# Reordered first loads, single stores of q and k, and earlier weight slices in an adaLN transformer block

## The chip, the cores and the metric

The kernel runs on one core of one Trainium2 chip. Its time is the device time of one execution in microseconds. The core has five engines that run their own instruction streams: TensorE (PE in the profile; PEld is its weight load), VectorE (DVE), ScalarE (ACT), GpSimd (POOL) and SyncE (SP), which here issues all DMAs, in order.

## The reference

One block with adaptive layer norm: six modulation rows are made from a condition vector c. Attention with 32 heads of 16 follows, and a dense layer pair with Mish between. All is float32, with S = 2048 rows of D = 512.

```python
mod = (_silu(c) @ w_mod).reshape(c.shape[0], 6, 1, -1)
sa, ca, ga, sb, cb, gb = (mod[:, i] for i in range(6))      # written out in the original
h = _layernorm(x) * (1 + ca) + sa
x = x + ga * attention(h, wqkv, wo)      # softmax(q k^T * 16**-0.5) v, then @ wo
h = _layernorm(x) * (1 + cb) + sb
x = x + gb * dense(h, w1, b1, w2)        # (v * tanh(softplus(v))) @ w2 with v = h @ w1 + b1
```

## The kernel before

**Precision.** Most products are made from split operands: each factor is a high part (rounded to the matmul format, `hi_copy`) and a low part (the rest, `lo_sub`), and three products hi x hi, hi x lo and lo x hi are summed (`mm3`). `h_h` and `h_l` are the two parts of the normalised input, transposed; `wh` and `wl` those of a weight slice; `qh` and `ql` those of a q or k unit.

**The start** (lines 329 to 514). x is 16 tiles of 128 rows, or four blocks (`tb`) of 512 rows. SP loads c, the first two 512-column parts of w_mod (`wma`, 1 MB each), x tiles 0 to 3, a 128-column weight slice of k and one of q, and then the other x tiles with the v slice among them. `sil` is silu(c). TensorE multiplies it with `wma` (line 449), ScalarE copies the result, and 16 matmuls with one column each (line 455, against `sel`) sum it into `modc`, which holds shift and scale per feature. The layer norm of a block is: statistics on VectorE (`stats_tb`, lines 374 and 375; `first_norm` for block 0), a few small operations on GpSimd, the scaling of x in place on ScalarE (`apply_tb`, line 385), transposes on TensorE and then, in `tr_tb`, `h_h` from PSUM on ScalarE (line 440), the same value in full precision, `hf`, on VectorE (line 441), and `h_l` as their difference (line 101) on VectorE or GpSimd (`LOV` says which). For each block the k unit of heads 0 to 7 follows (for block 0 the q unit too), with its matmuls against `h_l` last; for blocks 1 and 2 two v units as well. ScalarE casts the v weight slice (line 94) ahead of that.

**The way through memory.** A q or k unit (`qk_unit`, 8 heads by 512 rows) is written to HBM, to `qscr` and `kscr`, in the layout that the score matmuls read. For each of the 16 features of a head q has the three rows hi, hi, lo, and k has hi, lo, hi, so that one matmul over 48 rows makes the sum of three products. Two more rows of q hold a shift by the row maximum (`mt`, line 577), set to zero at first (`constants`). So q takes 50 rows and k 48 rows a head. A k unit is stored with two DMAs (512 and 256 KB), a q unit with three of 256 KB. `load_q` and `load_k` fetch a pair of heads into rows 0 and 64 of a `qa` and a `ka` tile, with one DMA per head each; there are five tiles of each (`NR`).

**The steps.** After that an order written out by hand runs in steps t = -20 to 511 and half steps h = 2t. Hooks (`at(h, f)`) put loads, stores and small operations at half steps. An iteration n is 16 steps: four heads (pairs 2n and 2n+1) against 512 query rows. The row maxima of a pair (lines 553 and 555 in the first 20 steps, 539 and 541 later) run 20 steps ahead of its scores (line 588), exponentials (591) and products with v (606; one group of eight instructions a step). Units of q, k and v of other heads, and later the dense layers, fill TensorE beside that. Pair 2n+1 is loaded at h = 32(n-1), when the tile that it takes comes free, and its first maxima come at step 16n - 12, which is four steps later. Pairs 2 and 3 are loaded at h = -22 and -8.

**Early weight slices.** `early_prep` loads six 256 KB slices of w1, splits them on GpSimd and stores both parts in HBM (`w1scr`); the six are loaded at h = 3i - 37, split 7 and stored 10 half steps later. GpSimd also splits the q and k weight slices and q and k units of that stretch.

`free_banks` tells the scheduler which instructions on different PSUM banks do not depend on each other, by the tile names that they touch.

## Time and profile before

| | us |
|---|---|
| three runs | 1690.85, 1691.66, 1695.13 (median 1691.66) |
| the profiled execution | 1691.02 |
| its span in the trace | 1689.2 |
| TensorE busy in the span | 1667.3 |
| VectorE, ScalarE, GpSimd busy | 1441.5, 1355.1, 821.1 |

Times in the trace count from the start of the span. A busy TensorE is not TensorE at its peak, since matmuls are pipelined. A row of the trace in order of time has the start, the length, the engine, the line, the operation with its tiles (written <- read) and shapes, a count where equal rows were merged, and, in brackets, how long the engine was idle before and what released it. "SPq" rows are DMA issues: their length is the time that SP took to issue, not the transfer's.

### The profile page before, as it was taken

The page shows a single profiled execution, that of the slowest core. Times are in us where ns is not written, and L with a number is a line of the kernel's source. Part 1 is how long each engine was busy: PE and PEld are TensorE (multiplying, and loading weights), DVE is VectorE, ACT ScalarE, POOL GpSimd, SP SyncE. Part 2 cuts the span into 40 slices and gives each one's busy share as a digit, 9 for nine tenths or more (in the row PEclk, how much of TensorE's full clock was granted, in tenths as well). Part 3 has the DMA queues.
Part 4 walks back from the last instruction along what each step waited for, and adds up shares of the span by engine and source line. Part 5 has one row for each costly group of instructions (what it writes and reads, how often), then busy time and mean ns, then how long its engine had stood idle before and what let it go on. Part 6 is the DMA issues. An engine that isn't in the chain of part 4 may idle for free.

```text
span 1689.2 us, 33772 instructions
## 1 busy us (share of the span) xinstructions
PE 1667.3 (99%) x12418; PEld 921.5 (55%) x12418; DVE 1441.5 (85%) x2369; ACT 1355.1 (80%) x2612; POOL 821.1 (49%) x843
## 2 busy tenths in 40 slices
PE   7999999999999999999999999999999999999999
PEld 5755655555444455555555455555555455555687
DVE  8898888888989988888889888888889888883377
ACT  6257777777778998888888998888888998889674
POOL 7555224655313564556323564556323565555442
PEclk9999999999999999999999999999999999999999
DMA  7877556777755443434355434534354533533261
GB/s 248 269 244 199 147 150 185 218 223 216 231 142 146 110 94 98 117 88 129 84 137 152 115 77 93 139 77 127 87 144 122 130 94 77 144 107 132 75 230 63
DMA packets 115406, 238.98 MB, mean 141 GB/s; under 512 B 24928, under 2 KB 50544, under 8 KB 109288
## 3 DMA queue, kind: packets, MB, share of 16 engines
q1 hardware_dynamic: 115240, 236.82, 49.9%
q8 instruction: 98, 1.61, 0.4%
q14 instruction: 68, 0.56, 0.1%
HBM read 180.48 MB, written 51.45 MB: 137 GB/s over the span
## 4 chain that ended last, share of the span: by engine, by line
PE 91%; DVE 3%; ACT 3%; DMA 2%; POOL 1%; issue 1%; SPq 0%; ACTq 0%; DVEq 0%; POOLq 0%
PE bk L606 29%; PE ring L588 22%; PE ring L539 20%; PE bk L139 11%; PE bk L132 3%; PE ring L1219 2%; PE ring L132 2%; DVE mx L541 2%; ACT pr L591 1%; PE ring L553 0%; DMA qa<-mt 0%; DMA xt<-in_A_x 0%; PE ring L922 0%; DMA kscr<-qh 0%; PE ring L568 0%
## 5 line engine op out<-in xcount | busy, mean ns | idle before, releaser
L541 DVE TENSOR_REDUCE mx<-ring 128x1 f32<-128x512 f32 x1968 | 1223.1, 682 | 150.0 <-PE ring L539 136.4
L591 ACT ACTIVATE pr<-ring 128x512 f32<-128x512 f32 x2048 | 1078.4, 603 | 207.1 <-PE bk L139 124.7
L539 PE MATMUL ring<-ka,qa 64*128 64x512 f32 x1968 | 817.9, 429 | 1.4 <-ACT pr L591 1.1
L588 PE MATMUL ring<-qa,ka 64*128 64x512 f32 x2048 | 759.1, 402 | 3.4 <-ACT pr L591 1.9
L606 PE MATMUL bk<-pr,vg 128*32 128x512 f32 x4096 | 545.1, 604 | 0.0
L539 PEld LDWEIGHTS ring<-ka,qa 64*128 64x128 f32 x1968 | 350.5, 184 | 326.2 <-DVE mx L541 251.3
L588 PEld LDWEIGHTS ring<-qa,ka 64*128 64x128 f32 x2048 | 373.7, 184 | 194.7 <-DVE mx L541 111.4
L139 PE MATMUL bk<-h,w 64*128 64x512 f32 (+1 forms) x1080 | 278.1, 390 | 0.0
L139 PE MATMUL bk<-w,a_h 64*128 64x512 f32 x632 | 210.9, 413 | 0.0
L139 PEld LDWEIGHTS bk<-h,w 64*128 64x128 f32 x1080 | 178.5, 184 | 9.3 <-ACT pr L591 1.5
L606 PEld LDWEIGHTS bk<-pr,vg 128*32 128x32 f32 x4096 | 81.2, 108 | 135.4 <-issue 126.0
L139 PE MATMUL bk<-w,a_l 64*128 64x512 f32 x316 | 124.0, 392 | 0.0
L139 PEld LDWEIGHTS bk<-w,a_h 64*128 64x128 f32 x632 | 106.8, 184 | 4.3 <-ACT hb L800 1.0
L978 POOL TENSOR_TENSOR y<-yd,y 128x512 f32<-128x512 f32 x44 | 56.9, 1293 | 89.0 <-ACT yd L977 79.7
L812 POOL TENSOR_SCALAR qq<-ee 128x512 f32<-128x512 f32 x25 | 15.5, 619 | 169.6 <-ACT ee L806 169.6
L828 POOL TENSOR_TENSOR qq<-qq,rr 128x512 f32<-128x512 f32 x42 | 54.1, 1289 | 85.9 <-ACT rr L822 85.9
L814 POOL TENSOR_TENSOR hb<-hb,ee 128x512 f32<-128x512 f32 x42 | 54.1, 1288 | 79.6 <-DVE ee L810 77.7
L139 PE MATMUL bk<-w,o_hl 64*128 64x512 f32 x288 | 79.1, 405 | 0.0
L101 POOL TENSOR_TENSOR a_l<-hb,a_h 128x512 fp32r<-128x512 f32 x53 | 73.1, 1379 | 4.4
L98 POOL TENSOR_SCALAR qh<-qf 128x512 fp32r<-128x512 f32 x27 | 16.7, 619 | 90.8 <-ACT qf L262 69.4
L139 PEld LDWEIGHTS bk<-w,a_l 64*128 64x128 f32 x316 | 58.3, 185 | 3.4
L139 PE MATMUL bk<-h_h,wl 64*128 64x512 f32 x168 | 57.2, 420 | 0.2 <-ACT pr L591 0.2
(219 smaller groups left out, 1909.1 us busy)
## 6 DMA issues: line engine op xcount, KB each, us to landing
ka<-kscr SPq DMA_DIRECT2D x124, 384.0 KB
w<-w2scr SPq DMA_DIRECT2D x56, 512.0 KB
w<-w1scr SPq DMA_DIRECT2D x46, 512.0 KB
vg<-vscr SPq DMA_DIRECT2D x32, 552.0 KB
qa<-qscr SPq DMA_DIRECT2D x124, 100.0 KB
kscr<-qh SPq DMA_DIRECT2D x16, 512.0 KB
qscr<-qh SPq DMA_DIRECT2D x32, 256.0 KB
w2scr<-hl SPq DMA_DIRECT2D x14, 512.0 KB
```

What stands on the lines that cost most here:

```text
L101: (nc.gpsimd if eng == "p" else nc.vector).tensor_sub(lo, src, hi.bitcast(F32))
L132: nc.tensor.matmul(acc, l, r, start=start, stop=stop)
L139: i = nc.tensor.matmul(acc, l[64 * g:64 * g + 64], r[64 * g:64 * g + 64], start=start and not then, stop=bool(stop and then))
L539: nc.tensor.matmul(pm, qt[64 * s:64 * s + 64, qs * P:(qs + 1) * P], kt[64 * s:64 * s + 64, kb * TB:(kb + 1) * TB], start=True, stop=True)
L541: nc.vector.tensor_reduce(out=mxs[n][:, s, 4 * j + qs, kb:kb + 1], in_=pm, op=ALU.max, axis=AX.X)
L588: nc.tensor.matmul(p_, kt[64 * s:64 * s + 64, kc * P:(kc + 1) * P], qt[64 * s:64 * s + 64, :], start=True, stop=True)
L591: e = nc.scalar.activation(pr, p_, AF.Exp, scale=SCALE)
L606: nc.tensor.matmul(accs[n][32 * h:32 * h + 32, :], vgs[n][:, o:o + 32], pts.pop((t, h)), start=(kc == 0), stop=(kc == 15))
L814: (nc.vector if tail else nc.gpsimd).tensor_mul(hb, hb, ee)
L828: nc.gpsimd.tensor_mul(qq, qq, rr)
L978: nc.gpsimd.tensor_add(y[i], yd, y[i])
L1219: nc.tensor.matmul(po[i // 2][:, i % 2, :], l[:, s], w[:, r, :], start=(f == 0 and j == 0), stop=(f == FT - 1 and j == 2))
```

## The change

- x tiles 0 to 3 are loaded first, then w_mod in eight tiles of 256 KB with the k slice between its halves. c is loaded by ScalarE's queue as four rows and transposed by TensorE. The table load of ScalarE comes after that issue.
- TensorE runs 34 transposes of the identity into a spare bank ahead of the modulation sums, and four behind them (`keep_busy`).
- The modulation is summed over the four parts of c in PSUM (`mod_sums`), copied as a 128 x 128 tile, transposed, and its columns 0, 32, 64 and 96 are `modc` (`mod_cols`). `sel` goes.
- Statistics are made two tiles at a time (`stats_two`) for blocks 0 and 1. Tile 3 is scaled on GpSimd. The split of the k slice goes to ScalarE and VectorE, that of the q slice to GpSimd. The split of the v slice moves between the scalings of tiles 5 and 6. ScalarE writes the ones into `ka[0]` and `ka[1]`; the zeros of `qa` come in two parts.
- `hf` becomes (transposed x times scale) minus `h_h`, one VectorE operation that waits for `h_h`; `h_l` is that plus the shift, on VectorE for k of `LOV`, else on GpSimd. For block 0 `LOV` names two of the four parts instead of one.
- q and k are stored once: hi and lo rows alternate, 34 rows a head for q (with the two shift rows) and 32 for k, two DMAs a unit. `load_q` takes the 34 rows into rows 16 on and the 16 hi rows into rows 0 to 15; `load_k` takes each hi row twice into rows 16 to 47 and the 16 lo rows into rows 0 to 15. So each head takes four DMAs instead of two, eight a pair.
- `free_banks` tells the four blocks of `h_h` apart.
- The six early slices are loaded at h = 2i - 39, split 4 and stored 7 half steps later. Pair 3 is loaded at h = -2.

```diff
--- before.py
+++ after.py
...
-    LOV = ((1,), (), (1, 3), (1, 3))
+    LOV = ((2, 3), (), (1, 3), (1, 3))
...
-    nc.scalar.preload_act_table_set("natural_log_exp_and_others")
...
-    kscr = dram.tile([H, 48, S], F32, name="kscr")
-    qscr = dram.tile([H, 50, S], F32, name="qscr")
+    kscr = dram.tile([H, 32, S], F32, name="kscr")
+    qscr = dram.tile([H, 34, S], F32, name="qscr")
...
-    sel = cst.tile([P, 1], F32, name="sel")
-    nc.gpsimd.memset(sel, 0.0)
-    for k in range(DK):
-        nc.gpsimd.memset(sel[32 * k:32 * k + 1, :], 1.0)
...
-                    names.add(v.tensor.name)
+                    part = v.offset % (DK * S) // TB if v.tensor.name == h_h.tensor.name else 0
+                    names.add((v.tensor.name, part))
                     if any(a is w for w in i.outs):
-                        made.add(v.tensor.name)
+                        made.add((v.tensor.name, part))
...
-            scr, rows = (qscr, 50) if kind == 0 else (kscr, 48)
+            scr, rows = (qscr, 34) if kind == 0 else (kscr, 32)
...
             def put():
                 put_away.add((kind, ct, tb))
                 o = 8 * ct * rows * S + tb * TB
-                if kind == 0:
-                    for r, src in enumerate((qh, qh, ql)):
-                        nc.sync.dma_start(dap(scr, o + r * S, [[rows * S, 8], [3 * S, DH], [1, TB]]), src.bitcast(F32))
-                    return
-                hi = qh.bitcast(F32)
-                twice = bass.AP(tensor=hi.tensor, offset=hi.offset, ap=[list(hi.ap)[0], [0, 2], [1, TB]])
-                nc.sync.dma_start(dap(scr, o, [[3 * S, P], [2 * S, 2], [1, TB]]), twice)
-                nc.sync.dma_start(dap(scr, o + S, [[3 * S, P], [1, TB]]), ql.bitcast(F32))
+                for r, src in enumerate((qh, ql)):
+                    nc.sync.dma_start(dap(scr, o + r * S, [[rows * S, 8], [2 * S, DH], [1, TB]]), src.bitcast(F32))
...
@@ -310,16 +300,20 @@
         qt = qa[pp % NR].bitcast(F32)
         assert (0, h // 8, qb) in put_away, (pp, put_away)
         for s in range(2):
-            nc.sync.dma_start(qt[64 * s:64 * s + rows, :], qscr[h + s, :rows, qb * TB:(qb + 1) * TB])
+            b, o = 64 * s, (h + s) * 34 * S + qb * TB
+            nc.sync.dma_start(qt[b + DH:b + rows, :], dap(qscr, o, [[S, rows - DH], [1, TB]]))
+            nc.sync.dma_start(qt[b:b + DH, :], dap(qscr, o, [[2 * S, DH], [1, TB]]))
 
     def load_k(pp, tb=None):
         n, j = divmod(pp, 2)
         h = 4 * (n % G) + 2 * j
         kt = ka[pp % NR].bitcast(F32)
-        at_ = slice(0, S) if tb is None else slice(tb * TB, (tb + 1) * TB)
+        at_, w = (slice(0, S), S) if tb is None else (slice(tb * TB, (tb + 1) * TB), TB)
         assert {(1, h // 8, i) for i in (range(NB) if tb is None else (tb,))} <= put_away, (pp, put_away)
         for s in range(2):
-            nc.sync.dma_start(kt[64 * s:64 * s + 48, at_], kscr[h + s, :, at_])
+            b, o = 64 * s, (h + s) * 32 * S + at_.start
+            nc.sync.dma_start(kt[b + DH:b + 48, at_], dap(kscr, o, [[2 * S, DH], [0, 2], [1, w]]))
+            nc.sync.dma_start(kt[b:b + DH, at_], dap(kscr, o + S, [[2 * S, DH], [1, w]]))
...
-        cc = lp.tile([P, DK], F32, name="cc")
-        nc.sync.dma_start(cc, c.rearrange("o (k p) -> p (o k)", p=P))
+        crow = lp.tile([DK, P], F32, name="crow")
+        nc.scalar.dma_start(crow, c.rearrange("o (k p) -> (o k) p", p=P))
+        nc.scalar.preload_act_table_set("natural_log_exp_and_others")
...
-        wma = [lp.tile([P, DK, D], F32, name=f"wma{i}") for i in range(2)]
-        for i in range(2):
-            nc.sync.dma_start(wma[i], w_mod[:, i * D:(i + 1) * D].rearrange("(k p) m -> p k m", p=P))
+        wma = [[lp.tile([P, D], F32, name=f"wma{i}{k}") for k in range(DK)] for i in range(2)]
+
+        def load_mod(i):
+            for k in range(DK):
+                nc.sync.dma_start(wma[i][k], w_mod[k * P:(k + 1) * P, i * D:(i + 1) * D])
+
         for t in range(4):
             load_x(t)
+        load_mod(0)
         slice_load(1, 0, lp, lp)
+        load_mod(1)
         slice_load(0, 0, lp, lp)
         for t in range(4, 8):
             load_x(t)
...
         zer = lp.tile([P, TB], F32, name="zer")
-        nc.gpsimd.memset(zer, 0.0)
-        for i in range(NR):
-            nc.gpsimd.memset(qa[i].bitcast(F32), 0.0)
-        for i in range(2):
-            nc.gpsimd.memset(ka[i].bitcast(F32), 1.0)
-
+        for t in qa[:3]:
+            nc.gpsimd.memset(t.bitcast(F32), 0.0)
+
+        spare = ring()
+
+        def keep_busy(n):
+            for _ in range(n):
+                nc.tensor.transpose(spare[:, :P], ident, ident)
+
+        keep_busy(8)
+        cc = ring()[:, :DK]
+        nc.tensor.transpose(cc, crow, ident[:DK, :DK])
+        keep_busy(26)
         e = lp.tile([P, DK], F32, name="sil_e")
         nc.scalar.activation(e, cc, AF.Exp, scale=-1.0)
         nc.vector.tensor_scalar_add(e, e, 1.0)
         nc.vector.reciprocal(e, e)
         nc.vector.tensor_mul(sil, cc, e)
+        hi_copy("a", ka[0], ones.to_broadcast([P, S]))
...
-        def first_norm():
...
+        def stats_two(q):
+
+            mv = lp.tile([P, 2, 2], F32, tag="ln_mv2", name="ln_mv2", bufs=2)
+            rs = lp.tile([P, 4, 2], F32, tag="ln_rs2", name="ln_rs2", bufs=4)
+            for i in range(2):
+                st_ = lp.tile([P, 6], F32, tag="ln_st", name="ln_st", bufs=4)
+                nc.vector.bn_stats(out=st_, in_=xts[2 * q + i])
+                nc.vector.bn_aggr(out=mv[:, i, :], in_=st_)
+                rss["x", 2 * q + i] = rs[:, :, i:i + 1]
+            nc.gpsimd.tensor_scalar(rs[:, 0, :], mv[:, :, 1], 1.0, EPS, op0=ALU.mult, op1=ALU.add)
+            nc.gpsimd.tensor_scalar(rs[:, 3, :], mv[:, :, 0], -1.0, 0.0, op0=ALU.mult, op1=ALU.add)
+            nc.gpsimd.tensor_tensor(rs[:, 1, :], rs[:, 0, :], nhalf.to_broadcast([P, 2]), op=ALU.pow)
+            nc.gpsimd.tensor_mul(rs[:, 2, :], rs[:, 3, :], rs[:, 1, :])
...
-            xt = xts[i]
+        def first_apply(i, eng="a"):
+            xt, rs = xts[i], rss.pop(("x", i))
             if eng == "a":
-                nc.scalar.activation(xt, xt, AF.Identity, scale=rs[:, 1, i:i + 1], bias=rs[:, 2, i:i + 1])
+                nc.scalar.activation(xt, xt, AF.Identity, scale=rs[:, 1, :], bias=rs[:, 2, :])
             else:
...
-        def first_tr():
...
+        pts = [bank(("ring", "ms", "ring", "acc")[k]) for k in range(DK)]
+        prs = [ring() for _ in range(2)]
+
+        def first_tr(i):
+            for k in range(DK):
+                nc.tensor.transpose(pts[k][:, i * P:(i + 1) * P], xts[i][:, k * P:(k + 1) * P], ident)
+
+        def mod_sums(i, ks):
+            for k in ks:
+                for m in range(DK):
+                    nc.tensor.matmul(prs[i][32 * m:32 * m + 32, :P], sil[:, k:k + 1].to_broadcast([P, 32]),
+                                     wma[i][k][:, m * P:(m + 1) * P], start=(k == 0), stop=(k == DK - 1))
+
+        def mod_cols(i):
+            row = lp.tile([P, P], F32, name=f"row{i}")
+            nc.vector.tensor_copy(row, prs[i][:, :P])
+            nc.tensor.transpose(prs[i][:, P:2 * P], row, ident)
+            cols = prs[i][:, P:2 * P:32]
+            if i:
+                nc.vector.tensor_scalar_add(modc[:, i, :], cols, 1.0)
+            else:
+                nc.vector.tensor_copy(modc[:, i, :], cols)
 
         def tr_tb(tb, ks=range(DK), pts=None):
             for k in ks:
@@ -438,36 +457,47 @@
                 hf = lp.tile([P, TB], F32, tag="hf", name="hf", bufs=6)
                 s = slice(tb * TB, (tb + 1) * TB)
                 nc.scalar.activation(h_h[:, k, s], pt, AF.Identity, scale=modc[:, 1, k:k + 1], bias=modc[:, 0, k:k + 1])
-                nc.vector.tensor_scalar(hf, pt, modc[:, 1, k:k + 1], modc[:, 0, k:k + 1], op0=ALU.mult, op1=ALU.add)
-                lo_sub("v" if k in LOV[tb] else "p", h_l[:, k, s], hf, h_h[:, k, s])
-
-        rs, hi_k = first_norm()
-        pr, pm = [], bank()[:, :2 * DK].rearrange("p (i k) -> p i k", k=DK)
-        for i in range(2):
-            pr.append(ring())
-            for k in range(DK):
-                nc.tensor.matmul(pr[i][32 * k:32 * k + 32, :], sil[:, k:k + 1].to_broadcast([P, 32]), wma[i][:, k, :],
-                                 start=True, stop=True)
-        for i in range(2):
-            row = lp.tile([P, D], F32, tag="hf", name="row", bufs=6)
-            nc.scalar.copy(row, pr[i])
-            for k in range(DK):
-                nc.tensor.matmul(pm[:, i, k:k + 1], row[:, k * P:(k + 1) * P], sel, start=True, stop=True)
-        for i in range(2):
-            first_apply(rs, i, "a")
-        split_lo(1, 0, hi_k)
-        hi_q = split_hi(0, 0, "a")
-        split_lo(0, 0, hi_q)
-        first_apply(rs, 2, "a")
-        first_apply(rs, 3, "v")
-        nc.vector.tensor_scalar_add(modc[:, 1, :], pm[:, 1, :], 1.0)
-        nc.vector.tensor_copy(modc[:, 0, :], pm[:, 0, :])
-        stats_tb(1)
-        tr_tb(0, pts=first_tr())
-        apply_tb(1)
+                nc.vector.scalar_tensor_tensor(hf, pt, modc[:, 1, k:k + 1], h_h[:, k, s].bitcast(F32), op0=ALU.mult,
+                                               op1=ALU.subtract)
+                if k in LOV[tb]:
+                    nc.vector.tensor_scalar_add(h_l[:, k, s], hf, modc[:, 0, k:k + 1])
+                else:
+                    nc.gpsimd.tensor_add(h_l[:, k, s], hf, modc[:, 0, k:k + 1].to_broadcast([P, TB]))
+
+        for q in range(2):
+            stats_two(q)
+        first_apply(3, "p")
+        for t in (*(t.bitcast(F32) for t in qa[3:]), zer):
+            nc.gpsimd.memset(t, 0.0)
+        mod_sums(0, (0, 1))
+        first_apply(0)
+        first_tr(0)
+        mod_sums(0, (2,))
+        first_apply(1)
+        first_tr(1)
+        mod_sums(0, (3,))
+        first_apply(2)
+        first_tr(2)
+        first_tr(3)
+        mod_cols(0)
+        hi_k = split_hi(1, 0, "a")
+        hi_copy("a", ka[1], ones.to_broadcast([P, S]))
+        split_lo(1, 0, hi_k, "v")
+        mod_sums(1, range(DK))
+        mod_cols(1)
+        keep_busy(4)
+        hi_q = split_hi(0, 0, "p")
+        split_lo(0, 0, hi_q, "p")
+        for q in range(2, 4):
+            stats_two(q)
+        tr_tb(0, pts=pts)
+        for i in range(4, 8):
+            first_apply(i)
+            if i == 5:
+                slice_split(2, 0, eng="v")
...
-                nc.sync.dma_start(dap(qscr, 48 * S + q4 * TB, [[50 * S, H], [S, 2], [1, TB]]), zer[:64, :])
...
         for tb in range(NB):
             if tb + 2 < NB:
                 stats_tb(tb + 2)
-            if tb == 0:
-                slice_split(2, 0, eng="v")
...
@@ -1465,11 +1493,11 @@
             for v, part in enumerate((hi, lo)):
                 nc.sync.dma_start(scr[:, v, :], part.bitcast(F32))
 
-        at(h + 7, split)
-        at(h + 10, put)
+        at(h + 4, split)
+        at(h + 7, put)
 
     for i in range(EARLY):
-        at(3 * i - 37, lambda i=i: early_prep(i, 3 * i - 37))
+        at(2 * i - 39, lambda i=i: early_prep(i, 2 * i - 39))
...
-    for pp, h in ((2, -22), (3, -8)):
+    for pp, h in ((2, -22), (3, -2)):
         at(h, lambda pp=pp: load_pair(pp))
```

31 lines of the change are left out of this document (5 added, 26 removed).

## The prediction

> **What bounds the kernel now.** I read the page first: the span, and the chain of work that ended last by engine.
>
> ```profile
> span 1689.2 us, 33772 instructions
> ...
> PE 91%; DVE 3%; ACT 3%; DMA 2%; POOL 1%; issue 1%; SPq 0%; ACTq 0%; DVEq 0%; POOLq 0%
> ```
>
> Nine tenths of the chain are TensorE (PE), so an edit can pay where PE waits for something else. The table of windows says where that is (columns: length, then busy time of PE, weight load, VectorE, ScalarE, GpSimd; granted clock, DMA share, GB/s).
>
> ```profile
> 10.00:20.00 10.00, 9.79 (x49) 7.09 (x41) 7.70 (x20) 4.74 (x8) 5.73 (x11) 1.00 1.07 393
> ...
> 20.00:50.00 30.00, 28.21 (x158) 22.27 (x156) 27.16 (x42) 23.25 (x36) 19.85 (x23) 1.00 0.62 190
> 50.00:102.00 52.00, 51.88 (x300) 36.85 (x302) 47.69 (x44) 9.84 (x22) 29.86 (x28) 1.00 0.89 281
> 102.00:1585.00 1483.00, 1476.55 (x11437) 774.91 (x11439) 1276.23 (x2153) 1259.15 (x2459) 721.20 (x717) 1.00 0.49 133
> ```
>
> From 102 us on, 512 steps take 1483 us, 2.9 us each, with DMA half busy. From 50 to 102 PE is full too. What the change rewrites is the first 50 us, which I read in order of time (start, length, engine, line, operation; in brackets the idle time before and its releaser).
>
> ```profile
> 1.32 0.16 DVE L80 TENSOR_REDUCE lows<-ident 32x1 f32<-32x16 f32 x1 [1.32 <-POOL ident masks.py:199]
> ...
> 3.17 0.20 ACT L361 ACTIVATE sil_e<-cc 128x4 f32<-128x4 f32 x1 [1.18 <-DMA cc<-in_c]
> ...
> 9.21 3.64 PE L449 MATMUL ring<-wma,sil 128*32 128x512 f32 x16 [9.21 <-DVE sil L364]
> 9.79 0.69 DVE L395 BATCH_NORM_STATS2 ln_st<-xt 128x6 f32<-128x512 f32 x1 [0.64 <-DMA xt<-in_A_x]
> ...
> 12.78 3.58 PE L455 MATMUL bk<-sel,row 128*128 128x1 f32 x16
> ...
> 16.52 0.15 DVE L463 TENSOR_SCALAR modc<-bk 128x4 f32<-128x4 f32 x1
> 16.66 0.68 DVE L374 BATCH_NORM_STATS2 ln_st<-xt 128x6 f32<-128x512 f32 x1
> ...
> 19.07 0.78 ACT L440 ACTIVATE h_h<-ring,modc 128x512 fp32r<-128x512 f32 x1 [2.93 <-PE ring L427]
> ...
> 22.23 2.94 ACT L385 ACTIVATE xt<-xt,ln_rs 128x512 f32<-128x512 f32 x4 [0.38 <-POOL ln_rs L379]
> 25.07 1.04 ACT L94 CAST wh<-wr 128x1024 fp32r<-128x1024 f32 x1
> 27.82 0.81 DVE L441 TENSOR_SCALAR hf<-ring,modc 128x512 f32<-128x512 f32 x1
> 29.43 5.06 POOL L101 TENSOR_TENSOR h_l<-hf,h_h 128x512 fp32r<-128x512 f32 x4
> 34.79 1.18 PE L132 MATMUL ring<-h_l,wh 128*128 128x512 f32 x4
> 50.34 0.73 PE L553 MATMUL ring<-ka,qa 64*128 64x512 f32 x4
> ```
>
> The first x tile arrives at 9.79, behind 2 MB of w_mod. The modulation runs through two matmul groups (9.21 to 12.85 and 12.78 to 16.36) to modc at 16.52; the first normalised block h_h starts at 19.07; the first maximum, where the regular steps begin, at 50.34. The time I predict is this last start, plus what changes behind it.
>
> **The change, part by part.**
>
> *Load order and modulation.* At 393 GB/s a 256 KB tile takes 0.67 us, and the first DMA issued was in use at 3.17. So x0 to x3, which now come first, land from about 3.5 to 5.5, the first MB of w_mod by 8.1, the k weight slice by 8.8, the second MB by 11.5, the q slice by 12.1: none of it behind its use below. PE gets 34 filler transposes ahead of the sums, then the first half's sums mixed with the 16 transposes of x, then the second half's sums. The fillers can start when the identity is built (1.3, row 1.32). What a transpose costs depends on when it runs:
>
> ```profile
> 17.33 0.42 PE L427 MATMUL bk<-ident,xt 128*128 128x128 f32 x1
> 17.54 0.42 PE L427 MATMUL ring<-ident,xt 128*128 128x128 f32 x1
> ...
> 25.39 0.60 PE L435 MATMUL bk<-ident,xt 128*128 128x128 f32 x4
> ```
>
> At 17 us they start 0.21 apart; at 25 us four take 0.60 in all, about 0.11 apart; the granted clock column shows 1.00 at both times. At the slow pace: fillers to 1.3 + 34 x 0.21 = 8.4, first sums 1.8 (half of 3.64), transposes 16 x 0.21 = 3.4, a row copy and its transpose 0.5, second sums 1.8, copy, transpose and add 1.1 (both estimated from rows 16.52 and 17.33 with the waits between engines): modc at 17.0, later than now. At the fast pace from 8.4 on: 0.9 + 1.7 + 0.5 + 0.9 + 1.1 gives modc at 13.5. I take 14.5 for the first h_h, nearer the fast row, since the fillers are a run of PE work as dense as the one ahead of 25 us: 4.6 us sooner (ends 2.0 and 5.5). [...]
>
> *What of the 4.6 us is left at 50.* ScalarE: four h_h (0.78 each), four applies (2.94) and the weight cast (1.04), which now stands in their middle: 14.5 + 3.1 + 4.0 = 21.6 against 25.17, 3.6 us sooner. VectorE: it starts the statistics of block 1 at 14.4 instead of 16.66, 2.2 us sooner, and then runs without a gap into hf of block 1 (27.82). The new fused hf has no row; its nearest ones:
>
> ```profile
> 19.88 0.81 DVE L441 TENSOR_SCALAR hf<-ring,modc 128x512 f32<-128x512 f32 x1
> ...
> 37.09 1.67 DVE L101 TENSOR_TENSOR h_l<-hf,h_h 128x512 fp32r<-128x512 f32 x1
> 38.68 0.68 DVE L101 TENSOR_TENSOR ql<-ring,qh 128x512 fp32r<-128x512 f32 x1
> ```
>
> It reads PSUM like both, with a scalar per partition like the first: 0.81 (lower end 0.68). The second step of h_l becomes an add from SBUF, 0.68 to 1.67 on VectorE in rows 38.68 and 37.09, perhaps less; block 0 has two of them there instead of one, so 0.7 of the 2.2 goes: hf of block 1 at 26.3. The fused hf also waits for h_h; behind it on VectorE stand the next hf and the statistics of a later block, and GpSimd's h_l waits for it. In block 0 VectorE comes to it at about 17.7, after h_h (from 14.5, one in 0.78), so the wait is covered by the statistics; with that cover gone it is 0.8 once a block. Block 1's four GpSimd adds (5.06) then end at 32.1 to 32.4 instead of 34.49. That is what the four matmuls at 34.79 need, so from there on PE is 2.1 to 2.4 us ahead, and blocks 2 and 3, whose work is unchanged in count, carry that to 50.34. **Term: -2.4**, ends -0.5 (h_h at 17.2) and -4.6 (VectorE's new operations shorter than the rows). At no cost: the ones for ka on ScalarE (two copies of twice the cast's width, 2.1 us each) in its idle time ahead of h_h, where one more than 1 us late would push h_h by as much; the zeros split in two runs on GpSimd, whose next due work is the q split; the finer key for bank dependences, since no row shows a wait that it removes.
>
> *Single stores, split loads.* Each k unit stores 512 KB instead of 768, each q unit two stores instead of three. Each pair load goes from four DMAs to eight, on SP alone, in order.
>
> ```profile
> 30.41 1.35 SPq L272 DMA_DIRECT2D qscr<-qh  x2
> ...
> 37.62 1.74 SPq L313 DMA_DIRECT2D qa<-qscr  x4
> 39.46 1.76 SPq L322 DMA_DIRECT2D ka<-kscr  x4
> 41.32 0.66 SPq L276 DMA_DIRECT2D kscr<-qh  x1
> ...
> 45.48 1.71 SPq L322 DMA_DIRECT2D ka<-kscr  x4
> ```
>
> 768 KB of q stores hold the q load for 7.2 us (30.41 to 37.62); 768 KB of k stores hold the k load for 4.2 (41.32 to 45.48). So q saves a third of that hold, some 2 us, and SP spends 0.44 us per issue: 3.5 more for the first two pairs' loads of a block. The k of the last block so goes out some 3 us later against PE, and the maxima first read it 12 steps after 50: covered; with that cover gone, it would be 3 us of PE.
>
> A gain further on, in the chain in order of time:
>
> ```profile
> 369.38 0.99 PE bk L606 x8
> ...
> 372.63 7.70 DMA qa<-mt
> ...
> 382.35 1.00 PE bk L606 x8
> ```
>
> and in SP's queue at that time:
>
> ```profile
> 371.83 3.34 SPq L577 DMA_DIRECT2D qa<-mt  x4
> ```
>
> Each step has one such L606 group, and these two are four steps apart: 12.97 us instead of 11.6, because the shift rows (mt) land 7.70 us after their issue began, behind q stores. One store fewer: **-1.1**, ends 0 and -1.4.
>
> The cost is in the loads. The second pair of each iteration is issued when its buffer comes free and is first read four steps (11.6 us) later. SP's queue near the second iteration, a line of SP's waits (who for whom, total, times, longest), and a piece of the chain much later:
>
> ```profile
> 146.52 0.67 SPq L313 DMA_DIRECT2D qa<-qscr  x2
> ...
> 153.89 2.83 SPq L272 DMA_DIRECT2D qscr<-qh  x2
> ```
>
> ```profile
> SPq L272 <- DMA ka<-kscr: 9.0, 7, 2.1
> ```
>
> ```profile
> 1313.28 5.04 DMA ka<-kscr
> ```
>
> Near 147 q stores waited for that k load, and the second was issued by 156.7; less its 0.6 us of issue, k landed about 9.6 us after 146.52: 2 us to spare. Near 1313 k took 5.04 from its issue, 6.5 with the issues ahead of it: 5 to spare. Four more issues add 1.8 us, and the q part of 34 rows may go slower than the 50 did (rival). I take three of the 30 pairs 0.7 us late: **+2.0**, ends 0 and 1 us on every pair, +30.
>
> *Early slices and pair 3.* The six loads, 12 stores and six splits (two operations of at most 1.3 us each on GpSimd, a quarter of row 29.43) come two to ten half steps sooner, behind the k loads of block 3 in SP's queue, and are meant to be done before the k units that end the stretch to 102 us; the load of pair 3 goes six half steps later, still five steps ahead of its first use. PE has no row of waiting for either: 0, bounds -0.7 and +1.5 (if GpSimd, waiting for a late slice, holds back the weight split queued behind it).
>
> Sum: -2.4 - 1.1 + 2.0 = **-1.5**. The profiled execution took 1691.02 us (span 1689.2), so 1689.5 by its measure; the median of the runs is 0.64 higher, so about **1690** as a median.
>
> **Rivals.** *Faster.* The whole head start stays (-4.6), the late shift rows are cured (-1.4), no load is late: 1691.7 - 6.0 = 1685.7. For it: ScalarE's path gains 3.6, and VectorE's fused operation may be 0.68. Against it: VectorE is busy 27.2 of the 30 us from 20 to 50, so its own work, which grows, sets the pace.
>
> *Slower: pair loads land after they are needed.* A q load of 34 rows would have to behave like the q stores above, which moved 768 KB in 7.2 us where k took 4.2, and delay the k parts behind it. Beyond 5 us of added delay (the room at 1313) every one of 30 pairs stalls PE; 0.4 us beyond is 12 us: 1691.7 - 3.5 + 12 = 1700. For it: 2 us of room near 147, no more. Against it: the q part is 68 KB beside 384. [...]
>
> *The fillers do not speed PE up*, so that part of the change does nothing: h_h at 17.2, -0.5 instead of -2.4: 1692.
>
> **How the numbers follow.** A measurement of this kernel can tell 0.3%, 5.1 us, from no change. Forecast 1690 (0.33) and weak fillers 1692 (0.07) lie within that; faster, 1685.7, has 0.34, because ScalarE's path alone would give 3.6 of it; late loads 0.26, because the room is as small as 2 us in one row. The range goes from 1684 (the faster case, a little more) to 1700 (late loads by 0.4 us on each pair); more lateness than that, 0.15, is left out. The likeliest case alone: 1687 (first term -4, loads 0) to 1695 (first term -0.5, loads +5).
>
> **What would show it.** Right: first use of x near 4 us, first h_h near 14.5, transposes of x 0.11 apart, first maximum near 48, steps of 2.9 us after that with no wait of PE for ka or qa, and no 7.7 us piece of qa<-mt. Wrong: a first maximum at or before 46 (faster); in the chain of waits "DMA ka<-kscr" or "DMA qa<-qscr" every 46 us, ahead of PE L539 (late loads); GpSimd waiting long for ep while ScalarE or PE waits for wl or ql (early slices).

## The result and the profile after

The changed kernel takes 1714.14 us as a median of five runs (1711.75 to 1718.04), against 1691.66 (1690.02 to 1695.13) for the kernel before: ratio 1.0129, 95% interval 1.0110 to 1.0149. I had forecast 1690 and a range up to 1700. The profiled execution of the changed kernel took 1718.04, its span 1716.3, so it stands at the slow end of its runs; the traces show 27.0 us of difference where the medians show 22.5. Line numbers moved: the maxima of the first 20 steps are L581 now, later ones L567 and L569, scores L616, products with v L634.

The page of the changed kernel, span and chain:

```profile
span 1716.3 us, 34291 instructions
...
PE 86%; DMA 6%; DVE 2%; ACT 2%; POOL 1%; issue 1%; SPq 1%; POOLq 0%; ACTq 0%; DVEq 0%
```

The windows of the changed kernel, cut as those of before:

```profile
10.00:20.00 10.00, 8.01 (x72) 5.11 (x70) 5.26 (x14) 7.11 (x10) 5.11 (x12) 1.00 1.07 372
20.00:50.00 30.00, 27.41 (x157) 21.81 (x158) 25.18 (x45) 21.44 (x33) 15.41 (x22) 0.94 0.52 148
50.00:102.00 52.00, 45.57 (x258) 32.42 (x257) 39.69 (x38) 7.55 (x18) 21.81 (x21) 0.93 0.74 222
102.00:1585.00 1483.00, 1464.50 (x11259) 770.50 (x11259) 1279.19 (x2152) 1238.43 (x2416) 714.15 (x709) 1.00 0.51 130
```

The stretch that I counted as unchanged, 50 to 102, has lost 6.3 us of TensorE's time (45.57 busy instead of 51.88), and its DMA share fell from 0.89 to 0.74. Up to 75 transfers were not in the way, they were not issued: the share is 0.46 from 50 to 62 and 0.64 from 62 to 75, before it was 0.58 and 1.02. From 90 to 102 it is 0.96 again. The granted clock of TensorE fell as well: 0.94 and 0.93 in the two middle windows, where before has 1.00. The start, in order of time:

```profile
1.34 1.97 PE L361 MATMUL ring<-ident 128*128 128x128 f32 x8 [1.34 <-POOL ident masks.py:199]
...
3.44 3.76 PE L361 MATMUL ring<-ident 128*128 128x128 f32 x26
...
4.25 0.68 DVE L401 BATCH_NORM_STATS2 ln_st<-xt 128x6 f32<-128x512 f32 x1
...
8.71 0.27 PE L431 MATMUL bk<-ident,xt 128*128 128x128 f32 x1
8.82 0.27 PE L431 MATMUL ring<-ident,xt 128*128 128x128 f32 x1
...
14.91 0.78 ACT L459 ACTIVATE h_h<-ring,modc 128x512 fp32r<-128x512 f32 x1 [1.76 <-DVE modc L445]
...
27.74 0.72 DVE L460 SCALAR_TENSOR_TENSOR hf<-ring,modc,h_h 128x512 f32<-128x512 f32 x1
...
47.69 0.73 PE L581 MATMUL ring<-ka,qa 64*128 64x512 f32 x4
```

The prologue did what it should: the first maximum starts at 47.69 instead of 50.34. Then SP falls behind. Its queue, then GpSimd and TensorE, in order of time on each, and the window behind TensorE's wait:

```profile
61.62 0.37 SPq L267 DMA_DIRECT2D kscr<-qh  x1
62.10 0.37 SPq L267 DMA_DIRECT2D kscr<-ql  x1
63.74 0.55 SPq L315 DMA_DIRECT2D ka<-kscr  x1
...
67.97 0.58 SPq L316 DMA_DIRECT2D ka<-kscr  x1
68.59 0.42 SPq L230 DMA_DIRECT2D wr<-in_A_wqkv  x1
69.12 2.10 SPq L1486 DMA_DIRECT2D ep<-in_B_w  x4
...
72.49 0.63 POOL L93 TENSOR_SCALAR ep<-ep 128x512 fp32r<-128x512 f32 x1 [16.93 <-DMA ep<-in_B_w]
...
83.73 1.26 POOL L96 TENSOR_TENSOR ep<-ep 128x512 fp32r<-128x512 f32 x1
84.95 1.26 POOL L96 TENSOR_TENSOR wl<-wr,wh 128x512 fp32r<-128x512 f32 x1
...
79.10 0.73 PE L127 MATMUL bk<-h_h,wh 128*128 128x512 f32 x2
86.27 2.08 PE L127 MATMUL bk<-h_h,wl 128*128 128x512 f32 x4 [6.43 <-POOL wl L96]
...
84.00:90.00 6.00, 3.73 (x10) 2.33 (x10) 0.04 (x1) 0.00 (x0) 4.08 (x4) 0.50 0.93 273
```

The same place of SP's queue in the kernel before:

```profile
58.59 1.99 SPq L322 DMA_DIRECT2D ka<-kscr  x4
...
61.19 1.54 SPq L1458 DMA_DIRECT2D ep<-in_B_w  x3
```

SP puts out eight k loads of block 3 (63.74 to 68.55), one by one at 0.52 to 0.58 us, and only then the first early slices (ep), at 69.12; before it was 61.19, behind four loads in 1.99 us. GpSimd takes its work in order: it stands 16.93 us for ep, then splits six slices in a row, and only then the weight slice wl (84.95) that TensorE wants. TensorE stands 6.43 us, and that costs more than its length: from 84 to 90 the granted clock is 0.50, and the four matmuls at 86.27 take 2.08 us where the four of the same form at 82.38 before take 1.09. The chain of waits goes on through transfers, in order of time; by itself it does not say which of them are late because SP was:

```profile
78.52 4.42 DMA ep<-in_B_w
...
87.69 8.04 DMA ka<-kscr
95.80 7.34 DMA qscr<-ql
...
109.87 8.59 DMA qa<-qscr
118.48 6.75 DMA wm<-in_w_mod
...
143.01 8.40 DMA ka<-kscr
...
396.93 7.16 DMA qa<-mt
...
427.40 9.67 DMA qa<-qscr
```

Worked out from the first L606 or L634 group of each iteration in the two traces: the first group is 8.4 us later than before (117.38 instead of 108.95; 11.1 lost since the first maximum), iteration 0 loses another 8.4, iteration 1 4.1, iterations 5 and 6 together 3.6, iteration 16 1.2, no other more than 0.4. Of 27.0 us 20.9 lie before 224, not in each of the 30 pairs.

### The profile page after: what moved, and what is told of

It is laid out like the page before. It is cut to its first block, busy times and chain, and to the rows that moved or that the text cites. A ratio compares the mean times of both kernels' runs of the same rounds, so it can differ in the third digit from the quotient of the medians.

```text
span 1716.3 us, 34291 instructions
## 1 busy us (share of the span) xinstructions
PE 1680.7 (98%) x12491; PEld 930.1 (54%) x12491; DVE 1433.4 (84%) x2372; ACT 1359.9 (79%) x2612; POOL 813.9 (47%) x839
## 4 chain that ended last, share of the span: by engine, by line
PE 86%; DMA 6%; DVE 2%; ACT 2%; POOL 1%; issue 1%; SPq 1%; POOLq 0%; ACTq 0%; DVEq 0%
PE bk L634 28%; PE ring L616 21%; PE ring L567 18%; PE bk L134 11%; PE ring L127 2%; PE ring L1247 2%; PE bk L127 2%; DVE mx L569 2%; DMA ka<-kscr 1%; ACT pr L619 1%; DMA qa<-qscr 1%; DMA sm<-ot 1%; DMA wm<-in_w_mod 1%; DMA ep<-in_B_w 0%; PE ring L950 0%
## 5 line engine op out<-in xcount | busy, mean ns | idle before, releaser
L569 DVE TENSOR_REDUCE mx<-ring 128x1 f32<-128x512 f32 x1968 | 1223.0, 682 | 159.6 <-PE ring L567 141.2
L567 PE MATMUL ring<-ka,qa 64*128 64x512 f32 x1968 | 821.2, 430 | 7.2 <-DMA ka<-kscr 3.7
L616 PE MATMUL ring<-qa,ka 64*128 64x512 f32 x2048 | 761.8, 403 | 8.3 <-DVE mx L569 5.0
L634 PE MATMUL bk<-pr,vg 128*32 128x512 f32 x4096 | 546.7, 606 | 0.0
L567 PEld LDWEIGHTS ring<-ka,qa 64*128 64x128 f32 x1968 | 351.6, 184 | 332.9 <-DVE mx L569 252.4
L616 PEld LDWEIGHTS ring<-qa,ka 64*128 64x128 f32 x2048 | 374.6, 185 | 198.6 <-DVE mx L569 119.6
L634 PEld LDWEIGHTS bk<-pr,vg 128*32 128x32 f32 x4096 | 81.4, 108 | 136.3 <-issue 127.1
L840 POOL TENSOR_SCALAR qq<-ee 128x512 f32<-128x512 f32 x25 | 15.6, 623 | 169.3 <-ACT ee L834 169.3
```

What stands on the lines that cost most here:

```text
L567: nc.tensor.matmul(pm, qt[64 * s:64 * s + 64, qs * P:(qs + 1) * P], kt[64 * s:64 * s + 64, kb * TB:(kb + 1) * TB], start=True, stop=True)
L569: nc.vector.tensor_reduce(out=mxs[n][:, s, 4 * j + qs, kb:kb + 1], in_=pm, op=ALU.max, axis=AX.X)
L616: nc.tensor.matmul(p_, kt[64 * s:64 * s + 64, kc * P:(kc + 1) * P], qt[64 * s:64 * s + 64, :], start=True, stop=True)
L634: nc.tensor.matmul(accs[n][32 * h:32 * h + 32, :], vgs[n][:, o:o + 32], pts.pop((t, h)), start=(kc == 0), stop=(kc == 15))
```

## The experiments

Theory: twice the issues per pair load hold back what stands behind them on SP, and parts on few DMA engines land late. Rivals: the early slices' dates, pair 3, or the new layout of the stores. How few shows in the DMA share, of 16 engines: while a pair's q parts of 34 and 16 rows are all that moves, it is 0.13 (592.10 to 593.10 in the changed kernel, 51 GB/s), some two engines; with q stores alone in the kernel before 0.52 (33 to 36, 184 GB/s), some eight; with k stores alone 1.03 (43.40 to 44.40, 389 GB/s), all of them. Medians are compared with the kernel before in the same session (1691.0 to 1692.5).

**Three parts alone, and one undone.** `order_only` is the changed kernel with the diffs of stores, loads, early slices and pair 3 undone. `stores_only` is the kernel before with the diffs of `kscr`, `qscr`, `put`, `load_q`, `load_k` and `constants`. `early_only` is before with

```diff
-        at(h + 7, split)
-        at(h + 10, put)
+        at(h + 4, split)
+        at(h + 7, put)
-        at(3 * i - 37, lambda i=i: early_prep(i, 3 * i - 37))
+        at(2 * i - 39, lambda i=i: early_prep(i, 2 * i - 39))
-    for pp, h in ((2, -22), (3, -8)):
+    for pp, h in ((2, -22), (3, -2)):
```

and `a_early_old` is the changed kernel with its first four lines turned back.

> The changed kernel with only its load order, fillers and fused split kept; stores, pair loads, early slices and the load of pair 3 as before. If the loss comes from SP's queue (theory: twice the issues per pair load hold back all that stands behind them), this part alone keeps its head start: first maximum near 47.7 and a median of 1689 to 1691, 1 to 2.7 us under the kernel before. If the new prologue itself crowds the stretch behind it (rival: TensorE comes 2.6 us sooner, the loads don't), the first pv group still starts at or after 109 and the time is 1692 or more.

> The kernel before with only the single stores and the split pair loads. SP theory: nearly the whole loss is here, 1709 to 1718; the early slices' loads are issued near 69 instead of 61, GpSimd waits for them some 15 us and TensorE stands still near 80. If the loss needs the early slices' new dates or the later load of pair 3 (rivals), this one is at 1690 to 1697.

> The kernel before with only the early slices' new dates and the later load of pair 3. SP theory: SP is free by 61 here, the slices land in time, so 1690 to 1694. Rival (GpSimd takes up the splits too early and waits in order, with the weight split queued behind): 1697 to 1705, with a wait of GpSimd for ep of 5 us or more near 62.

> The changed kernel with the early slices' old dates alone (later by 2 to 10 half steps; split 7 and store 10 half steps behind the load). Rival of the early dates: TensorE's stand near 80 goes, 1700 to 1706. SP theory: the loads still go out near 69, behind the k loads of block 3; the later split lets the weight split pass, so part of the first 11 us comes back, but the pair loads stay late: 1706 to 1714.

| kernel | median us | ratio to before, 95% interval |
|---|---|---|
| order_only | 1690.56 | 0.9992 (0.9983 to 1.0001) |
| stores_only | 1716.60 | 1.0137 (1.0123 to 1.0151) |
| early_only | 1692.03 | 1.0003 (0.9993 to 1.0012) |
| a_early_old | 1710.90 | 1.0112 (1.0098 to 1.0126) |

The whole loss is in the stores and loads. The dates alone cost nothing. In the changed kernel they lengthen TensorE's first stand: with the old dates (`a_early_old`) it is 2.09 us instead of 6.43.

```profile
81.26 2.08 PE L127 MATMUL bk<-h_h,wl 128*128 128x512 f32 x4 [2.09 <-POOL wl L96]
```

The load order alone gains at most a little: its first maximum came at 46.35, 4.0 us sooner than before, but its first product with v at 108.3, only 0.7 sooner. Its windows show where the rest went (same columns as above):

```profile
66.00:96.00 30.00, 29.88 (x153) 19.62 (x151) 27.69 (x28) 5.35 (x12) 20.64 (x21) 1.00 1.02 317
96.00:102.00 6.00, 4.10 (x19) 2.67 (x17) 3.87 (x5) 1.55 (x4) 1.89 (x2) 0.84 0.89 318
102.00:108.00 6.00, 5.39 (x33) 3.47 (x32) 4.85 (x9) 4.98 (x11) 2.53 (x3) 0.87 1.01 326
```

From 66 on DMA is full (1.02), and between 96 and 102 TensorE is busy 4.10 of 6 us. In its chain of waits the pieces of that time are transfers:

```profile
90.86 6.88 DMA ka<-kscr
97.81 3.39 DMA kscr<-qh
```

TensorE runs ahead of the transfers and waits for them.

**Which part of the stores and loads.** `split_loads` keeps the double stores and the wide rows of before and only cuts the loads. `q_only` and `k_only` give the new stores and loads to one of the two (rows of q and k then stand in different orders, so the scores differ from the reference's; work and transfers are those named). `q_32_2` is `stores_only` with 34 rows cut in two:

```diff
-            nc.sync.dma_start(qt[b + DH:b + rows, :], dap(qscr, o, [[S, rows - DH], [1, TB]]))
+            for a, z in ((DH, 48), (48, rows))[:1 + (rows > 48)]:
+                nc.sync.dma_start(qt[b + a:b + z, :], dap(qscr, o + (a - DH) * S, [[S, z - a], [1, TB]]))
```

> The kernel before with its double stores and wide scratch rows, only each pair load issued in two parts with the changed kernel's shapes (k 32 and 16 rows, q 34 and 16). Theory: the loads' issues cost the time, not the stores: 1708 to 1718, SP still in the k loads of block 3 near 69. Rival: what costs is the single stores' layout (loads that pick every second row, or read one row twice): 1690 to 1697.

> The kernel before with single stores and split loads for q alone; k as before. If the part of 34 rows is what lands late (its DMA took 10 us near 82 where 50 rows took 6), most of the loss is here: 1704 to 1714. If it is SP's issue time in blocks 0 to 3 (q has 4 more there, k 16 more): 1692 to 1697.

> The kernel before with single stores and split loads for k alone; q as before. SP issue time: 1702 to 1712, GpSimd's first ep still past 70. 34 rows of q: 1690 to 1697.

> The kernel before with single stores and split loads, and the 34 rows of q cut into 32 and 2, one issue more for each head. If the slow landing of 34 rows is the price: 1698 to 1708, against 1716.6 without the cut, although SP issues more. If the number of issues is the price: 1716 to 1722.

| kernel | median us | ratio to before, 95% interval |
|---|---|---|
| split_loads | 1738.17 | 1.0283 (1.0266 to 1.0300) |
| q_only | 1700.71 | 1.0060 (1.0042 to 1.0078) |
| k_only | 1705.02 | 1.0086 (1.0071 to 1.0102) |
| q_32_2 | 1702.94 | 1.0071 (1.0056 to 1.0086) |

Both are true, each for its half: k's loads cost 14 us, q's 10. The split by itself, with the old stores, costs 47; far past what I expected, and the single stores give some 22 of it back. The split itself does not make an issue dearer: in three of the four blocks eight k issues of `split_loads` took about 3.6 us, 0.45 each, where those of the changed kernel took 0.60 from one to the next.

```profile
59.21 3.58 SPq L324 DMA_DIRECT2D ka<-kscr  x8
```

Cutting 34 rows into 32 and 2 gains 11 us by the ratios and 14 by the medians, although SP issues more. Worked out from the semaphore updates in the two traces, the median time from issue to landing is 5.5 us for the 34 rows of `stores_only` and 2.2 for the 32 rows of `q_32_2`; the 32-row k part of a pair, issued behind them, lands after 7.7 and 4.8. The chain of `stores_only` has these pieces, that of `q_32_2` none of them between 60 and 125:

```profile
81.74 7.84 DMA qa<-qscr
...
103.26 6.56 DMA qa<-qscr
...
110.72 4.09 DMA qa<-mt
```

**In the whole change, and another layout.** `a_q_32_2` makes the same cut in the changed kernel. `before_q48`, `order_q48` and `order_single_q32` take the two zero rows out of the scratch, so that no large part of q has to go on few DMA engines:

```diff
-    qscr = dram.tile([H, 50, S], F32, name="qscr")
+    qscr = dram.tile([H, 48, S], F32, name="qscr")
...
-                    for r, src in enumerate((qh, qh, ql)):
-                        nc.sync.dma_start(dap(scr, o + r * S, [[rows * S, 8], [3 * S, DH], [1, TB]]), src.bitcast(F32))
...
+                hi, n = qh.bitcast(F32), kind + 1
...
+                nc.sync.dma_start(dap(scr, o, [[3 * S, P], [n * S, 2], [1, TB]]), twice)
+                nc.sync.dma_start(dap(scr, o + (2 - kind) * S, [[3 * S, P], [1, TB]]), ql.bitcast(F32))
...
-            nc.tensor.matmul(pm[:, s, :], qt[64 * s:64 * s + 64, qs * P:(qs + 1) * P],
-                             kt[64 * s:64 * s + 64, kb * TB:(kb + 1) * TB], start=True, stop=True)
+            nc.tensor.matmul(pm[:, s, :], qt[64 * s:64 * s + 48, qs * P:(qs + 1) * P],
+                             kt[64 * s:64 * s + 48, kb * TB:(kb + 1) * TB], start=True, stop=True)
```

This is `before_q48`; `order_q48` has it on top of `order_only`. In `order_single_q32`, made from `a_early_pair3_old` below, q has 32 rows like k, each store covers `[[2 * S, P], [1, TB]]`, and a q load takes 32 and 16 rows. With the zero rows other things go too: the four stores of zeros, one of the three stores of a q unit in the first two kernels, and a quarter of the rows that the maxima multiply. These runs do not separate that from the number of engines.

> The whole changed kernel with one edit: the 34 rows of each q load go out as 32 and 2. If the causes found in the single stores (slow 34 rows, 13.7 us there) stand in the whole change too: 1714 - 13.7 = 1700, 1697 to 1704. If the early slices' new dates have made another wait the first one: 1706 to 1714.

> The kernel before with q's scratch at 48 rows instead of 50: the two zero rows are neither stored nor loaded, the maxima multiply 48 rows of each head instead of 64 (the shift rows are left out by that). So q is stored like k (hi twice by one DMA, on all engines) and loaded as 48 rows. If the few engines of the q stores and of the 50 rows hold up the stretch from 66 to 108: 1684 to 1690. If they are covered: 1691 to 1693.

> The same q scratch of 48 rows on top of the new load order, with the stores, k loads, early slices and pair 3 as before. The new order's first maximum was 4.0 us sooner, and 3.3 of that were lost again between 96 and 108 with DMA share near 1.0. If q's DMAs take less of it: 1685 to 1688, below both kernels. If the bytes alone set that stretch: 1689 to 1691.

> The changed kernel with the early slices and pair 3 as before, and no part on two engines: scratch of 32 rows for q as for k, no zero rows, the maxima over 48 rows, stores on all engines, pair loads of 32 and 16 rows (8 issues). What is left of the change's loss is SP's issues: k_only lost 14 us, q's issues add to that, the store bytes give some back: 1697 to 1706. If the two engines were all of it: 1686 to 1692.

| kernel | median us | ratio to before, 95% interval |
|---|---|---|
| a_q_32_2 | 1699.82 | 1.0047 (1.0032 to 1.0063) |
| before_q48 | 1691.11 | 1.0000 (0.9991 to 1.0009) |
| order_q48 | 1687.05 | 0.9973 (0.9963 to 0.9983) |
| order_single_q32 | 1699.27 | 1.0047 (1.0034 to 1.0061) |

In the changed kernel one edit at the 34 rows gives 14.3 us back, of 22.5. And `order_q48` beats both kernels, by 4.4 us against before: neither half does that alone (0.9992 and 1.0000). Its windows, beside those of `order_only`:

```profile
66.00:96.00 30.00, 29.88 (x153) 19.68 (x151) 27.70 (x28) 5.73 (x12) 18.16 (x20) 1.00 0.96 313
96.00:102.00 6.00, 5.62 (x36) 3.74 (x35) 5.85 (x8) 3.31 (x7) 2.97 (x3) 1.00 1.01 329
102.00:108.00 6.00, 5.77 (x45) 3.31 (x45) 5.27 (x10) 5.16 (x11) 3.88 (x3) 1.00 1.03 372
```

TensorE is busy 11.39 of the 12 us from 96 to 108 instead of 9.49. DMA is full (1.01 and 1.03) and moves 329 and 372 GB/s instead of 318 and 326.

**Where the rest is.** `k_split_blocks` and `k_split_late` are before with the k loads cut, the one in blocks 0 to 3, the other in whole pairs (`tb is None`):

```diff
-            nc.sync.dma_start(kt[64 * s:64 * s + 48, at_], kscr[h + s, :, at_])
+            for a, b in ((DH, 48), (0, DH)) if tb is not None else ((0, 48),):
+                nc.sync.dma_start(kt[64 * s + a:64 * s + b, at_], kscr[h + s, a:b, at_])
```

`blocks_on_act` issues the small k parts of blocks 0 to 3 on ScalarE's queue (`nc.sync` to `nc.scalar`), on top of `order_single_q32`. `order_q48_early` adds the early dates to `order_q48`. `a_early_pair3_old` is the changed kernel with early slices and pair 3 at the old dates.

> The kernel before (double stores, wide scratch) with only the k loads of the first two pairs, block by block, issued in two parts: 16 issues more, all between 38 and 70. If SP's issue time there is what delays the early slices and all behind them: 1698 to 1706. If the split costs by later loads: 1691 to 1694.

> The kernel before with only the k loads of whole pairs (from the third pair on) issued in two parts; those of the blocks as before. If the price lies in the first blocks: 1691 to 1695, with at most a stall near 390. If it lies with the later pairs, as my forecast had it: 1697 to 1706.

> As order_single_q32 (1699), but the 16 small parts of the first two pairs' k loads go out on ScalarE's queue instead of SP's. If SP's time holds back the early slices: GpSimd has its first ep 6 to 8 us sooner and the time is 1688 to 1694. If it is the number of DMAs or their bytes, whoever issues them: 1697 to 1702.

> As order_q48 (1687), with the early slices and the load of pair 3 at the changed kernel's dates. With SP free by 60 the dates should not matter: 1685 to 1689. If they cost by themselves when TensorE comes sooner: 1690 to 1694.

> The changed kernel with the early slices and the load of pair 3 both at the dates of before: the new load order plus single stores and split loads, nothing else. If the two parts add up (1690.6 and 1716.6 apart): 1713 to 1717. If the head start of the load order helps SP to get ahead of the early slices: 1707 to 1711. Against the 1710.9 with the early dates alone undone it also tells what the later load of pair 3 is worth here: theory none, within 2 us.

| kernel | median us | ratio to before, 95% interval |
|---|---|---|
| k_split_blocks | 1699.67 | 1.0050 (1.0035 to 1.0065) |
| k_split_late | 1697.95 | 1.0038 (1.0023 to 1.0053) |
| blocks_on_act | 1701.84 | 1.0063 (1.0046 to 1.0080) |
| order_q48_early | 1687.61 | 0.9977 (0.9967 to 0.9986) |
| a_early_pair3_old | 1716.03 | 1.0128 (1.0112 to 1.0145) |

The 16 issues in blocks 0 to 3 cost 8.0 us, the later ones 6.3; together 14.3 if they add up, as much as `k_only` lost (14.0). So k's saved bytes gave back nothing that shows, unless the dearer issues of `k_only` took it up; no run separates the two. GpSimd in `k_split_blocks`, then in `k_split_late`, and from the chain of the latter its largest later piece:

```profile
72.83 0.63 POOL L98 TENSOR_SCALAR ep<-ep 128x512 fp32r<-128x512 f32 x1 [14.72 <-DMA ep<-in_B_w]
```

```profile
65.17 0.63 POOL L98 TENSOR_SCALAR ep<-ep 128x512 fp32r<-128x512 f32 x1 [7.07 <-DMA ep<-in_B_w]
```

```profile
376.20 7.41 DMA qa<-mt
```

So SP's time in the blocks is what sends the early slices out late. In `k_split_late` 1.9 of the 6.1 us between the two traces are lost before the first product with v and 2.8 in iteration 5 (50.15 us, 47.36 before). There the wait for the shift rows, which was in the kernel before already, grows: TensorE stands 2.42 us instead of 1.24, and in the trace its clock is then halved for 3.4 us. `blocks_on_act` missed what I expected; its time lies where the rival had it, the number of DMAs, whoever issues them. What speaks for SP's time even so is where the time went. GpSimd has its slices sooner (last row; 69.98 in `order_single_q32`), but ScalarE now waits in SP's place:

```profile
51.75 0.59 ACT L89 CAST qh<-ring 128x512 fp32r<-128x512 f32 x1 [4.56 <-DMA ka<-kscr]
...
57.62 0.62 ACT L89 CAST wh<-wr 128x512 fp32r<-128x512 f32 x1 [5.29 <-DMA ka<-kscr]
...
64.79 0.62 POOL L93 TENSOR_SCALAR ep<-ep 128x512 fp32r<-128x512 f32 x1
```

From the first maximum to the first product with v it takes 64.3 us instead of the 69.0 of `order_single_q32`, but the first maximum comes at 51.0 instead of 46.1. Loads that wait for their store held the engine that issues them in both kernels: SP waits 6.9 us for kscr<-ql in the kernel before, in three waits ahead of k loads, and ScalarE gets to its k loads here only at 49.65 and 55.30, within the 4.56 and 5.29 us. The early dates changed nothing in `order_q48`. Inside the change the kernels with and without them (1714.1, 1710.9, 1716.0) are not told apart.

## Why the prediction was wrong

- **Load order and modulation, -2.4:** the size was met, the path only in part. Forecast were x at 4, `h_h` at 14.5, transposes 0.11 apart, the first maximum at 48; measured 4.25, 14.91, 0.11 (8.71 to 8.82) and 47.69, 2.65 sooner than before. By their starts in the trace the fillers run 0.21 us apart up to 4.77 and 0.11 apart from 4.96 on: TensorE does get faster under them, and the rival of weak fillers falls. The change of pace comes 3.6 us behind the first filler (1.34 to 4.96); in the kernel before the transposes at 17 still started 0.21 apart. No run shows an `h_h` at the 17.2 that the lower end and that rival were counted from; the slow pace ended at 4.96, and the first `h_h` came at 14.91. Within the term the path was another one: `hf` of block 1 started at 27.74, 0.1 sooner instead of 1.5, and the shorter operations (`hf` 0.72, GpSimd's adds 1.0 instead of 1.27) made up for a part. The four matmuls with `h_l` that stood at 34.79 came at 33.49, 1.3 us sooner, not 2.1 to 2.4. The other half of the gain came in blocks 2 and 3, where I had counted none, so that the sum came out right was in part luck. What I left out is that a head start at 48 is none at 108: in `order_only` the waits for DMA took back 3.3 of 4.0.
- **Late shift rows, -1.1:** wrong for the whole change. One q store fewer does cure them as long as k's loads stay whole: in `q_only` iteration 5 takes 46.08 us (47.36 before), and TensorE does not wait for them there. With k's loads split too it does not: TensorE waits 1.96 us for them in `stores_only` and 1.03 in the changed kernel, against 1.24 before. The 7.16 us at 396.93 are the length of the transfer and not its price. With k's split and the three stores of q it grows, to 3.02 in `k_only` and 2.42 in `k_split_late`. The rest of the changed kernel's long iteration 5 (49.81 us) is mostly a wait of 2.42 us at 378.51, behind the transfer of sm<-ot. In `order_q48`, with q in 48 rows and k's loads whole, iteration 5 takes 46.19. These are single traces, and the wait also moves with what came earlier: it is 0.39 us in `k_split_blocks`, whose later loads are those of before.
- **Split loads, +2.0:** this is the step that failed, in size and in place. Stores and loads alone cost 24.3 us (`stores_only`); of the 22.5 of the changed kernel 14.3 go with the 34 rows (last point) and some 8 stay. I looked for late pairs among the 30 later ones, where three were to be 0.7 us late; 20.9 of 27.0 us were lost before 224. I had noted "SP spends 0.44 us per issue" and that the k of the last block goes out "some 3 us later", covered by 12 steps. An issue took 0.52 to 0.58, the eight k issues of a block 4.8 to 5.0 us instead of 1.7 to 2.0 for four, and what stood behind them on SP was not the k of the last block but wr, ep, the stores and the next pairs, 7.9 us late at 69.12. I priced the moved loads by their reader and not by the queue behind them.
- **Early slices, 0 with +1.5 at most:** the mechanism was named ("GpSimd, waiting for a late slice, holds back the weight split queued behind it"), and it is what TensorE's first stall shows, but with 6.43 us. SP's delay and the new dates make it together: with the old dates 2.09 us of it are left, and without the delay the dates cost nothing (`early_only` 1692.0).
- **The slower rival:** a q load of 34 rows that behaves like the q stores, on few engines (shares of 0.13 and 0.52 above), was the right mechanism for 14 of the 22.5 us. I set it aside because "the q part is 68 KB beside 384". The size was not what counted. The k parts behind the 34 rows did land late, as the rival had it, but not on each of 30 pairs: against `a_q_32_2` the trace of the changed kernel loses 2.1 us before the first product with v, 10.8 in iterations 0 and 1 and 3.4 in 5 and 6. The semaphore updates go with the shares: in the changed kernel the semaphore of a load of 34 rows is raised three times, that of a 32-row or 16-row load sixteen times; in the kernel before a q store raises it nine times and a load of 50 rows eleven times, a k store and a load of 48 rows, the forms that `order_q48` has for q too, sixteen times. Three updates go with two engines and nine with eight; that eleven go with ten is an estimate from those two pairs.

What stays open: why the split costs 47 us with double stores and 24 with single ones. Of the difference between the two traces 4.7 us lie before the first product with v and 15.6 in iterations 3 to 7. k's single stores gave nothing back that shows, so it should be q's, whose third store goes; no run kept the loads cut and changed q's stores alone. Open is also how the 8 us that the whole change still loses without its 34 rows divide between SP's issues in the blocks and later ones, and how much of each wait is the halved clock behind it.

## What to carry to other kernels

An issue cost more here than the time until its reader: price it by everything queued behind it on the issuing engine (7.9 us on SP here), and by the in-order engines that wait for those (GpSimd 16.93, TensorE 6.43). Before counting a transfer's bytes, look at how many DMA engines it keeps busy: here 34 rows landed in 5.5 us and 32 of them, cut off, in 2.2. A head start paid here only with the next crowded resource relieved as well: the load order and the 48-row scratch gained nothing measurable apart and 4.4 us together.

## What was new about the hardware

- An issue of SP for a k part took 0.52 to 0.58 us in the changed kernel; whole loads of 48 rows took 0.43 to 0.50 before (1.71 to 1.99 for four), and the parts of `split_loads`, cut alike from plain rows, mostly 0.45. So the dearer issue goes with k's new layout and not with the cut. Why is open: q's 16 rows, which also pick every second row, took 0.42 in three issues of four at 36 to 40 us.
- A load of 68 KB in 34 rows took a median of 5.5 us from issue to landing (`stores_only` and the changed kernel), and 6.6 to 10.2 in the chains of these kernels between 80 and 118 us; 32 rows took 2.2 (`q_32_2`), and cut into 32 and 2 the load was not the piece that the chain waited for there.
- A wait of TensorE cost more than its length. Behind the 6.43 us at 80 the granted clock was 0.50 (84 to 90), and four matmuls took 2.08 us instead of 1.09. Over the whole trace it was 0.993 to 0.996 in the five runs of the changed kernel and 0.999 to 1.00 in the eight of `order_q48`, whose trace has no such wait.
- Bytes saved on the way to HBM (47.25 MB written in `k_only`, 51.45 before) gave nothing that shows in the time; splitting the loads for it cost 14 us.
